# The bucket hash of an attention kernel: one fp32 product on the turned block in place of three split products, and the value product in three parts

## The chip, the cores and the metric

One Trainium2 chip, one core. The time is the device time of one execution in microseconds (us); the kernel before takes 741.85 us, the median of three runs (741.52 to 741.86).

## The reference

Two stages. The first is an attention for 2 batches of 8 heads, 768 positions and 64 columns, in which a query sees only the keys of its own hash bucket:

```python
q_bits = (np.einsum('bhsd,dk->bhsk', q, proj) > 0)          # proj is 64 x 6
k_bits = (np.einsum('bhsd,dk->bhsk', k, proj) > 0)
q_bucket = np.sum(q_bits * 2 ** np.arange(6), axis=-1)       # k_bucket likewise
mask = q_bucket[:, :, :, None] == k_bucket[:, :, None, :]
scores = np.where(mask, q @ k.T / 8, -1e9)
attn = exp(scores - max);  attn = attn / (sum(attn) + 1e-9)
out = attn @ v
```

The second stage takes its output as x (1536 x 512) through 4 experts: `out += p[:, e] * (relu(x @ w1[e]) @ w2[e])`, with w1 512 x 1024 and w2 1024 x 512. Everything is fp32, and the kernel keeps near fp32 by splitting each operand into a high part of reduced precision (fp32r) and the rest, and adding up three products.

## The kernel before, in words

**Order of the work.** Heads are numbered 0 to 15 over both batches. Attention is written as a software pipeline: a step handles 128 queries of one head, so a head has six steps t = 0 to 5, and in step i the stages of several earlier steps are issued in the order of the string `ORDER = "TXSUVMEYNRP"`. The first batch's attention runs alone on the engines (heads 0 to 7, and head 8 with it), then the experts of batch 0 run on TensorE with the attention of batch 1 spread between them, then the experts of batch 1 alone. Each engine executes its own instructions strictly in this written order, and the SP queue issues nearly all transfers in order.

**Stages.** S (`stage_s`): four fp32r matmuls give the scores of 128 queries against 768 keys (`sps`, two banks from the pool `big` with two buffers); VectorE (DVE) takes the row minimum out of them into `p`. E: ScalarE (ACT) takes the exponent. For heads 0 to 8 (`mixed`) T turns `p` with six TensorE transposes into `ptps` (pool `one`, four buffers of one bank), which ACT and DVE copy out; for heads 9 to 15 X and Y turn it by DVE block transposes and a trip through DRAM. V (`stage_v`, L509) multiplies with v: fp32 matmuls, two at a time side by side in the array (`tile_position=(0, g * D)`), into `pv`. U copies `pv` out, M (GpSimd, POOL) applies the denominators. N takes the reciprocal of the denominators `den`, to which E's last step has added 1e-9 on ACT (L410). `LAG_V` says how many steps behind a head's last step V runs: for mixed heads in two parts, at lags 4 and 6 (t = 3 and t = 5 of the next head), for the others in one part at lag 7.

**Preparing a head.** While head x is in work, the generator `prep_head` (from L292) prepares head x+1, one piece per step, at the end of the step (P). It starts from q and k turned so that the 64 columns of q and the 64 of k lie on the 128 partitions. For most heads (`BLOCKS`) DVE does the turning from 32x32 blocks (`turn_blocks`, L288, result `xt`), for heads 0, 1, 9 and 10 TensorE. Then `split_half`: ACT makes the high part `ah` (L230), DVE the rest `al` (L231). POOL copies pieces of these into `q1` and `k2` (L221). TensorE computes the **hash** (L329) as three split products, each in two halves of 384 columns: six matmuls into `hps`, which takes one of the two `big` buffers that the scores use:

```python
for j, (w, a) in enumerate(((phi, ah), (plo, ah), (phi, al))):
    for i, sl in enumerate(halves):
        nc.tensor.matmul(ps[i][:MKE, :NH], w, a[:, sl], start=j == 0, stop=j == 2)
```

ACT takes the sign (L316), POOL makes bit vectors of it (L343) and copies them (L221); they are extra rows of `al` and `k2`, so that the score product itself adds a huge number wherever a bit differs. The first product of head x+1 therefore waits for POOL's last copy. For mixed heads the split is in step t = 0, the hash in t = 2, sign and bits in t = 3.

**Weights.** `load_w` loads expert weights through two buffers on the SP queue, `split_w` splits them (DVE L683, POOL L676), already during the first batch.

Of the kernel before, what the change touches and what calls it, by code (L numbers as in the profile page):

```python
# [18 lines left out]
SGN_SCALE = float(2**20)  # L19
ATT_PACE = 1.0  # L20
LAG_E = 1
LAG_N = 3
LAG_R = ((6, 4), (7, 6))
LAG_T = 3
LAG_X = 2
LAG_Y = 4
LAG_V = ((4, 6), (7,))
LAST_V = (4, 5)
LAG_U = (3, 1)
LAG_M = (10, 10)  # L30
PP_BUFS = 6
TW = 3
QK_AT = 1
BLOCKS = (2, 3, 4, 5, 6, 7, 8, 11, 12, 13, 14, 15)
W_LOAD = 14
W_BUFS = 2
WC = 2
# [12 lines left out]
def tile_lsh_attention__then__domain_moe(  # L50
# [59 lines left out]
    pr = const.tile([P, 2, NB], F32, name="pr")  # L110
    phi_t = const.tile([P, P], F32R, name="phi")
    plo_t = const.tile([P, P], F32R, name="plo")
    phi, plo = phi_t[:, :MKE], plo_t[:, :MKE]
    eps = const.tile([P, 1], F32, name="eps")
# [33 lines left out]

    def setup():
        nc.vector.memset(warm, 0.0)  # L150
        nc.vector.memset(eps, 1e-9)
        nc.scalar.activation(warm[:, 0:1], warm[:, 0:1], ACTF.Exp)
        make_identity(nc, ident)
        keep_warm(N_WARM)
        step_column(qk_scale, ((0, -scale), (D, 1.0)))
        step_column(
            sgn_bias, ((0, -TINY), (MQ + NB, TINY), (MQE, 0.0), (MK, TINY), (MK + NB, -TINY), (MKE, 0.0))
        )
        step_column(bit_mul, ((0, 0.5), (MK, BIG / 2)))
        nc.vector.memset(phi_t.bitcast(F32), 0.0)  # L160
        nc.vector.memset(plo_t.bitcast(F32), 0.0)
        for i, s in ((0, -1.0), (1, 1.0)):
            hi, lo = (
                x[:, MQ:P].rearrange("p (a n) -> p a n", a=2)[:, :, i * NB : (i + 1) * NB] for x in (phi_t, plo_t)
            )
# [21 lines left out]
    def in_blocks(b, h):  # L187
        return b * H + h in BLOCKS
# [100 lines left out]

    def prep_head(b, h):  # L290
        second = (b, h) == (0, 1)
        if not second and not in_blocks(b, h):  # L292
            tqk = loaded.pop((0, b, h))
        q1, al, ah, k2 = stack_tiles(b, h)
        if second:
            for ps, sl in zip(in_psum, halves):
                split_half(ah[:, sl], al[:, sl], ps[:, :NH])
        elif in_blocks(b, h):
            if (b, h) not in xts:
                turn_blocks(b, h)  # L300
                yield 0
            split_half(two(ah), two(al), two(xts.pop((b, h))))
        else:
            ps = big("tps")
            for c in range(NT):
                nc.tensor.transpose(
                    ps[:, c // 3, (c % 3) * P : (c % 3 + 1) * P], tqk[:, c].rearrange("p a d -> p (a d)"), ident
                )
            split_half(two(ah), two(al), ps[:, :, :NH])
        for rows in (slice(0, D), slice(D, P)):  # L310
            copy_pool(q1[rows], ah[0:D].bitcast(F32))
        copy_pool(k2[0:D], ah[D:P].bitcast(F32))
        yield 654

        def sign():
            nc.scalar.activation(  # L316
                two(k2[D:MKE]), hps[D:MKE, :, :NH], ACTF.Sign, bias=sgn_bias[D:MKE], scale=SGN_SCALE
            )

        if mixed(b, h) and (second or in_blocks(b, h)):  # L320
            yield 0
        if second:
            ps = [one("hps1") for _ in range(2)]
        else:
            hps = big("hps")
            ps = [hps[:, i] for i in range(2)]
        for j, (w, a) in enumerate(((phi, ah), (plo, ah), (phi, al))):
            for i, sl in enumerate(halves):
                nc.tensor.matmul(ps[i][:MKE, :NH], w, a[:, sl], start=j == 0, stop=j == 2)  # L329
        copy_pool(ah[0:D], al[D:P].bitcast(F32))  # L330
        if second:
# [4 lines left out]
        if not mixed(b, h):  # L336
            sign()
        yield 978
        if b and h and not in_blocks(b, h):
            yield 0  # L340
        if mixed(b, h) and not second:
            sign()
# [9 lines left out]
        yield 0  # L352

    xhi = {}
    xlo = {}
# [46 lines left out]
    def stage_e(b, h, t):  # L402
        pt, nb = probs_t[b, h, t]
        r, o, n = span_of(b, h, t)
        if o == 0:
            dens[b, h, r] = sm.tile([P, NT], F32, tag="den", name="den")
        nc.scalar.activation(pt, pt, ACTF.Exp, bias=nb, scale=-1.0, accum_out=dens[b, h, r][:, o : o + 1])  # L407
        if o == n - 1:
            den = dens[b, h, r][:, :n]
            nc.scalar.activation(den, den, ACTF.Identity, bias=eps)  # L410

    rdbs = {}
    rows = {}
# [1 line left out]
    def stage_n(b, h, t):  # L415
        r, o, n = span_of(b, h, t)
        if o != n - 1:
            return
        den = dens.pop((b, h, r))
        rd = sm.tile([P, NT], F32, tag="rd", name="rd", bufs=2)  # L420
        nc.vector.reciprocal(out=rd[:, :n], in_=den[:, :n])
        rows[b, h, r] = dr.tile([P, n], F32, tag=f"row{n}", name="row", bufs=6)
        nc.sync.dma_start(out=rows[b, h, r], in_=rd[:, :n])
# [149 lines left out]
    def attention():  # L573
# [3 lines left out]
        def do(op, i):  # L577
# [10 lines left out]
            elif op == "T":  # L588
                j = i - LAG_T
                if 0 <= j < n and heavy(*seq[j]):  # L590
                    stage_t(*seq[j])
                    return 654
            elif op == "X":
                j = i - LAG_X
                if 0 <= j < n and not heavy(*seq[j]):
                    stage_x(*seq[j])
            elif op == "Y":
                j = i - LAG_Y
                if 0 <= j < n and j % G == G - 1 and not heavy(*seq[j]):
                    b, h, t = seq[j]  # L600
                    stage_y(b, h, t // G)
            elif op == "S":
                if i < n:
                    b, h, t = seq[i]
                    if t == 0:
                        x = hseq.index((b, h))
                        prep[0] = prep_head(*hseq[x + 1]) if x + 1 < len(hseq) else iter(())
                    stage_s(b, h, t)
                    return 652 + 4270 // NT
                return DRAIN  # L610
            elif op == "V":
                for bh, lag in ended(i):
                    for part, at in enumerate(v_lags(*bh)):
                        if lag == at:
                            stage_v(*bh, part, len(v_lags(*bh)))
            elif op == "U":
                for bh, lag in ended(i):
                    if lag == u_lag(*bh):
                        stage_u(*bh)
            elif op == "M":  # L620
                for (b, h), lag in ended(i):
                    for g in range(NT // G):
                        if h % 2 and lag == (u_lag(b, h) if (b, h) == (0, H - 1) else LAG_M[b] + g):
# [434 lines left out]
```

## Time and profile before

| | |
|---|---|
| median of three runs | 741.85 us |
| the profiled execution | 741.69 us |
| its span, first to last instruction | 740.0 us |
| TensorE (PE) busy | 720.4 us, 97% of the span |
| DVE, POOL, ACT busy | 474.5, 306.3, 298.9 us |
| mean granted TensorE clock | 0.992 |
| attention of batch 0 and head 8 | to about 152 us |
| experts of batch 0 with attention of batch 1 | 152 to 430 us |
| experts of batch 1 | 430 to 740 us |

A busy share is an average over these three stretches. PE's matmuls are pipelined and their ends are modelled, so durations of PE work are best read from the start of one group to the start of the next. "Idle before" and "waited for" say what an engine stood still for, and what ended it.

### The profile page before, as it was taken

Reading aid. Unit: us, or ns where it says so; the run is one execution under the profiler, and the core shown is the slowest. Engines: PE = TensorE matmul, PEld = TensorE weight load, DVE = VectorE, ACT = ScalarE, POOL = GpSimd, SP = SyncE. Lnnn points to the kernel's source line nnn. Section 1 sums busy time; section 2 is a strip of 40 time slices with the busy share of each in tenths; the row PEclk is TensorE's granted clock in tenths of the full one; section 3 lists DMA queues with packets and bytes.
Section 4 is the critical chain, followed back from the end, with each engine's and each line's share of the span. In section 5 each row is a group of like instructions: output and inputs, shape, how many; then the busy total and the mean of one; then the engine's idle time right before and its main releaser. Section 6 shows DMA issues by size and latency. Waiting matters only on the chain.

```text
span 740.0 us, 10166 instructions
## 1 busy us (share of the span) xinstructions
PE 720.4 (97%) x3826; PEld 618.4 (84%) x3826; DVE 474.5 (64%) x781; ACT 298.9 (40%) x592; POOL 306.3 (41%) x279
## 2 busy tenths in 40 slices
PE   8898889999999999999999999999999999999997
PEld 6666666698897897979779799998989989899896
DVE  6677776545776666667553334798668686676863
ACT  6676767643242241523312010443435334353440
POOL 5338585442335441644132324844234242343420
PEclk9999999999999999999999999999999999999999
DMA  6233324302877797789668211242121221212202
GB/s 143 44 65 66 79 43 101 74 13 69 208 203 177 216 229 189 194 209 280 173 196 231 83 58 57 72 157 85 48 67 58 85 86 34 81 57 78 93 0 86
DMA packets 85504, 83.05 MB, mean 112 GB/s; under 512 B 49872, under 2 KB 52432, under 8 KB 85456
## 3 DMA queue, kind: packets, MB, share of 16 engines
q1 hardware_dynamic: 84432, 82.08, 41.0%
q8 instruction: 30, 0.49, 0.3%
q10 hardware_dynamic: 1024, 0.33, 0.2%
q14 instruction: 18, 0.15, 0.1%
HBM read 62.68 MB, written 19.71 MB: 111 GB/s over the span
## 4 chain that ended last, share of the span: by engine, by line
PE 91%; ACT 4%; DVE 4%; issue 0%; DMA 0%; POOL 0%; DVEq 0%; POOLq 0%
PE mps L715 12%; PE mps L716 12%; PE mps L717 12%; PE pv L509 9%; PE mps L776 6%; PE mps L775 6%; PE mps L777 6%; PE sps L384 3%; PE sps L386 3%; PE ptps L454 3%; PE hps L329 3%; PE mps L930 2%; PE mps L926 2%; PE mps L929 2%; DVE al L231 2%; PE pd L926 2%
## 5 line engine op out<-in xcount | busy, mean ns | idle before, releaser
L715 PE MATMUL mps<-w2hi,hh 128*128 128x512 f32 (+1 forms) x388 | 150.7, 388 | 0.0
L717 PE MATMUL mps<-w2hi,hl 128*128 128x512 f32 (+1 forms) x388 | 150.5, 388 | 0.0
L716 PE MATMUL mps<-w2lo,hh 128*128 128x512 f32 (+1 forms) x388 | 150.4, 388 | 0.0
L391 DVE TENSOR_SCALAR_CACHE_REDUCE p<-sps 128x768 f32<-128x768 f32 x96 | 90.4, 943 | 34.0 <-PE sps L386 32.1
L407 ACT ACTIVATE p<-p,nb 128x768 f32<-128x768 f32 x96 | 89.4, 932 | 37.0 <-DVE p L391 36.5
L709 DVE SCALAR_TENSOR_TENSOR acc<-mps,pe,acc 128x512 f32<-128x512 f32 (+1 forms) x85 | 63.0, 742 | 63.1 <-PE mps L717 62.6
L781 ACT ACTIVATE hh<-mps 128x384 fp32r<-128x384 f32 x64 | 31.4, 490 | 162.3 <-PE mps L777 162.3
L776 PE MATMUL mps<-xs,w1hi 128*128 128x384 f32 x256 | 85.9, 336 | 0.6 <-POOL xs L554 0.6
L775 PE MATMUL mps<-xs,w1hi 128*128 128x384 f32 x256 | 86.4, 337 | 0.0
L777 PE MATMUL mps<-xs,w1lo 128*128 128x384 f32 x256 | 85.9, 336 | 0.0
L717 PEld LDWEIGHTS mps<-w2hi,hl 128*128 128x128 f32 x388 | 72.9, 188 | 15.6
L912 POOL TENSOR_TENSOR w2lo<-ws,w2hi 128x512 fp32r<-128x512 f32 x32 | 40.5, 1286 | 108.4 <-ACT w2hi L911 108.4
L716 PEld LDWEIGHTS mps<-w2lo,hh 128*128 128x128 f32 x388 | 72.9, 188 | 13.8
L715 PEld LDWEIGHTS mps<-w2hi,hh 128*128 128x128 f32 x388 | 72.8, 188 | 13.8
L676 POOL TENSOR_TENSOR w1lo<-ws,w1hi 128x512 fp32r<-128x512 f32 x32 | 42.6, 1332 | 88.3 <-DVE w1hi L683 58.8
L782 DVE SCALAR_TENSOR_TENSOR hl<-mps,hh 128x384 fp32r<-128x384 f32 x64 | 35.4, 555 | 66.6 <-ACT hh L781 66.4
L676 POOL TENSOR_TENSOR w2lo<-ws,w2hi 128x512 fp32r<-128x512 f32 x32 | 41.3, 1289 | 70.5 <-DVE w2hi L683 56.3
L509 PE MATMUL pv<-pt,tv 128*64 128x384 f32 x288 | 67.6, 492 | 0.0
L221 POOL TENSOR_SCALAR q<-ah 64x768 fp32r<-64x768 f32 (+1 forms) x33 | 32.2, 975 | 68.5 <-ACT ah L230 67.2
L384 PE MATMUL sps<-ah,q 128*128 128x384 f32 x192 | 54.6, 365 | 0.3 <-DVE p L391 0.3
L454 PEld LDWEIGHTS ptps<-ident,p 128*128 128x128 f32 x324 | 38.7, 145 | 16.3 <-issue 7.8
L871 POOL TENSOR_TENSOR w1lo<-ws,w1hi 128x512 fp32r<-128x512 f32 x24 | 37.1, 1551 | 36.4 <-ACT w1hi L867 22.7
(135 smaller groups left out, 1430.5 us busy)
## 6 DMA issues: line engine op xcount, KB each, us to landing
ws<-in_moe_w_dram SPq DMA_DIRECT2D x64, 512.0 KB, 4.0
scr<-t SPq DMA_DIRECT2D x14, 1152.0 KB, 8.9
pt<-scr SPq DMA_DIRECT2D x56, 288.0 KB, 6.1
tv<-in_v_dram SPq DMA_DIRECT2D x16, 192.0 KB, 4.3
out_dram<-acc SPq DMA_DIRECT2D x11, 256.0 KB, 2.0
rdb<-row SPq DMA_DIRECT2D x14, 192.0 KB, 5.3
tqk<-in_q_dram SPq DMA_DIRECT2D x26, 96.0 KB, 3.3
tqk<-in_k_dram SPq DMA_DIRECT2D x24, 96.0 KB, 3.4
```

Of the source, the lines that this page charges most:

```text
L384: nc.tensor.matmul(ps[:, i, :NH], q1[:, sl], k1[:, i * NH : (i + 1) * NH], start=True, stop=False)
L391: nc.vector.tensor_scalar(out=two(pt), in0=ps[:, :, :NH], scalar1=MASKED, scalar2=MASKED, op0=ALU.min, op1=ALU.min, accum_out=nb,)
L407: nc.scalar.activation(pt, pt, ACTF.Exp, bias=nb, scale=-1.0, accum_out=dens[b, h, r][:, o : o + 1])
L509: nc.tensor.matmul(dst, vvs[b, h][:, c], pts[b, h, g][c], start=c == 0, stop=c == NT - 1, tile_position=(0, g * D),)
L676: nc.gpsimd.tensor_tensor(out=lo[:, c - 1], in0=st[c - 1], in1=hi[:, c - 1].bitcast(F32), op=ALU.subtract)
L709: nc.vector.scalar_tensor_tensor(out=acc, in0=ps, scalar=pcol, in1=acc, op0=ALU.mult, op1=ALU.add)
L715: nc.tensor.matmul(ps, hh[:, ts], w2hi[:, f, cs], start=n == 0, stop=False)
L716: nc.tensor.matmul(ps, hh[:, ts], w2lo[:, f, cs], start=False, stop=False)
L717: nc.tensor.matmul(ps, hl[:, ts], w2hi[:, f, cs], start=False, stop=n == FC - 1)
L775: nc.tensor.matmul(ps[:, :SB], w1hi[:, kk, fs], xhi[b, kk][:, sl], start=kk == 0, stop=False)
L776: nc.tensor.matmul(ps[:, :SB], w1hi[:, kk, fs], xlo[b, kk][:, sl], start=False, stop=False)
L777: nc.tensor.matmul(ps[:, :SB], w1lo[:, kk, fs], xhi[b, kk][:, sl], start=False, stop=kk == KD - 1)
```

## The change

Five things, all around `prep_head`:

1. The hash of heads 2 to 15 is no longer made of `ah` and `al`, but in fp32 straight from `xt`, with weights `pf` (the projections times their signs and the scale, made once by POOL): two matmuls, one for each half of the columns, side by side in the array and in one bank of the pool `one`. The sign becomes two ACT instructions of 384 columns.
2. The pieces move: for mixed heads `ah` in t = 1, `al` in t = 2, hash, sign and bits in t = 3, the hash directly behind V; for the others `ah` in t = 0, `al`, hash and sign in t = 1, bits in t = 2. The turning on DVE is for all heads in the last step of the head before.
3. Heads 9 and 10 are loaded in blocks and turned by DVE, too.
4. V of mixed heads in three parts at lags 4, 6 and 8, that is in t = 3, 5 and 1; for the others at lag 8, with U at lag 9.
5. 1e-9 is added to the denominators on DVE in N, not on ACT in E.

```diff
+SPLIT_AT = (1, 0)
+HASH_AT = (3, 1)
-LAG_V = ((4, 6), (7,))
+LAG_V = ((4, 6, 8), (8,))
-LAG_U = (3, 1)
+LAG_U = (1, 1)
-BLOCKS = (2, 3, 4, 5, 6, 7, 8, 11, 12, 13, 14, 15)
+BLOCKS = tuple(range(2, 16))
...
+        nc.gpsimd.tensor_copy(sgn_bias[0 : MKE - D], sgn_bias[D:MKE])
+        nc.gpsimd.memset(pf, 0.0)
...
+            nc.gpsimd.tensor_scalar(
+                out=pf.rearrange("p (a n) -> p a n", a=2)[:, :, i * NB : (i + 1) * NB],
+                in0=pr, scalar1=qk_scale, scalar2=s, op0=ALU.mult, op1=ALU.mult,
+            )
...
+            xt = xts.pop((b, h))
+            for _ in range(SPLIT_AT[not mixed(b, h)]):
+                yield 0
+            nc.scalar.activation(two(ah), two(xt), ACTF.Copy, scale=qk_scale)
+            copies()
             yield 0
-        if mixed(b, h) and not second:
-            sign()
+            nc.vector.scalar_tensor_tensor(
+                out=two(al), in0=two(xt), scalar=qk_scale, in1=two(ah).bitcast(F32),
+                op0=ALU.mult, op1=ALU.subtract,
+            )
+            copy_pool(ah[0:D], al[D:P].bitcast(F32))
+            for _ in range(HASH_AT[not mixed(b, h)] - SPLIT_AT[not mixed(b, h)] - 1):
+                yield 0
+            hps = one("hps")
+            for i, sl in enumerate(halves):
+                nc.tensor.matmul(
+                    hps[i * D : i * D + MKE - D, :NH], pf[:, : MKE - D], xt[:, sl],
+                    start=True, stop=True, tile_position=(0, i * D),
+                )
+            for i, sl in enumerate(halves):
+                rows = slice(i * D, i * D + MKE - D)
+                nc.scalar.activation(
+                    k2[D:MKE, sl], hps[rows, :NH], ACTF.Sign, bias=sgn_bias[rows], scale=SGN_SCALE
+                )
...
-        if o == n - 1:
-            den = dens[b, h, r][:, :n]
-            nc.scalar.activation(den, den, ACTF.Identity, bias=eps)
+        nc.vector.tensor_scalar(out=den[:, :n], in0=den[:, :n], scalar1=1e-9, scalar2=None, op0=ALU.add)
         nc.vector.reciprocal(out=rd[:, :n], in_=den[:, :n])
...
-                    if t == NT - 1 and x + 2 < len(hseq) and in_blocks(*hseq[x + 2]) and mixed(*hseq[x + 2]):
+                    if t == NT - 1 and x + 2 < len(hseq) and in_blocks(*hseq[x + 2]):
                         turn_blocks(*hseq[x + 2])
```

The order of TensorE's instructions around a hash of the first batch. Before, in step t = 2 and the next one (`ptps` are the transposes, `sps` the scores, `hps` the hash, `pv` the value product):

```order
L454 MATMUL ptps<-ident,p 128x128 x6
L384 MATMUL sps<-ah,q_372 128x384 x2
L386 MATMUL sps<-k_375,al 128x384 x2
L329 MATMUL hps<-ah,phi 108x384 x2
L329 MATMUL hps<-ah,plo 108x384 x2
L329 MATMUL hps<-al,phi 108x384 x2
L454 MATMUL ptps<-ident,p 128x128 x6
L384 MATMUL sps<-ah,q_372 128x384 x2
L386 MATMUL sps<-k_375,al 128x384 x2
L509 MATMUL pv<-pt,tv 64x384
L509 MATMUL pv<-pth,tv 64x384
```

Of the change, in step t = 3:

```order
L470 MATMUL ptps<-ident,p 128x128 x6
L402 MATMUL sps<-ah,q_374 128x384 x2
L404 MATMUL sps<-k_377,al 128x384 x2
L525 MATMUL pv<-pt,tv 64x384
L525 MATMUL pv<-pth,tv 64x384
L525 MATMUL pv<-pt,tv 64x384
L525 MATMUL pv<-pth,tv 64x384
L346 MATMUL hps<-xt,pf 44x384 x2
L470 MATMUL ptps<-ident,p 128x128 x6
```

Six matmuls that stood alone between two steps are two behind the four of V, and they read `xt` instead of `ah` and `al`.

The same on DVE, from the turning of the next head (`xt`) on. Before:

```order
L288 STREAM_TRANSPOSE xt<-tqk 128x768
L458 COPY pth<-ptps 128x3x128
L391 TENSOR_SCALAR p,nb<-sps 128x768
L231 SCALAR_TENSOR_TENSOR al<-xt,qk_scale,ah 128x768
L683 CAST w1hi<-ws 128x512
L391 TENSOR_SCALAR p,nb<-sps 128x768
L458 COPY pth<-ptps 128x3x128
L391 TENSOR_SCALAR p,nb<-sps 128x768
L536 COPY xf<-pv 64x384
L421 RECIPROCAL rd<-den 128x6
```

Of the change:

```order
L299 STREAM_TRANSPOSE xt<-tqk 128x768
L474 COPY pth<-ptps 128x3x128
L409 TENSOR_SCALAR p,nb<-sps 128x768
L699 CAST w1hi<-ws 128x512
L409 TENSOR_SCALAR p,nb<-sps 128x768
L474 COPY pth<-ptps 128x3x128
L409 TENSOR_SCALAR p,nb<-sps 128x768
L552 COPY xf<-pv 64x384
L436 TENSOR_SCALAR den<-den 128x6
L437 RECIPROCAL rd<-den 128x6
L333 SCALAR_TENSOR_TENSOR al<-xt,qk_scale,ah 128x768
```

`al` moved from behind the scores of t = 0 to behind everything of t = 2, and the small addition to `den` stands ahead of the reciprocal.

POOL's instructions of the change in steps t = 2 to 4 of a head with odd number:

```order
L232 TENSOR_SCALAR ah<-al 64x768
L692 TENSOR_TENSOR w1lo<-ws,w1hi 128x512
L565 TENSOR_TENSOR xf<-xf,rdb 128x384
L567 TENSOR_SCALAR xs_114<-xf 128x384
L570 TENSOR_TENSOR xs_114<-xf,xs_114 128x384
L361 TENSOR_SCALAR al<-k_711,bit_mul 44x768
L232 TENSOR_SCALAR k_711<-al 12x768
```

Their order is the one of before; what moved is the moment from which the first (it needs DVE's `al`) and the sixth (it needs the sign) can run.

## Rows read from the trace of the kernel before

**Rows 1.** Stretches: us, PE, PEld, DVE, ACT, POOL busy (instructions), clock, DMA share, GB/s
```profile
24.82:137.22 112.40, 102.61 (x626) 75.23 (x627) 78.12 (x150) 79.92 (x167) 65.29 (x69) 0.95 0.30 65
...
151.95:430.00 278.05, 278.05 (x1460) 238.94 (x1460) 165.23 (x287) 83.62 (x167) 102.61 (x92) 1.00 0.67 179
430.00:740.00 310.00, 306.19 (x1549) 277.84 (x1547) 205.94 (x290) 109.08 (x205) 117.95 (x81) 1.00 0.21 70
```

**Rows 2.** Waits of PE from 7 to 151 us: total us, times, longest
```profile
PE hps L329 <- DVE p L391: 9.3, 7, 2.1
PE ptps L454 <- ACT pth L460: 1.9, 6, 0.3
PE hps L329 <- DVE al L231: 0.8, 1, 0.8
```

**Rows 3.** The chain that ended last, around one hash: start, us, what
```profile
72.58 1.62 DVE al L231
74.20 0.75 DVE p L391
75.13 1.30 PE hps L329 x6
```

**Rows 4.** The same chain, from two hashes to the next value products
```profile
24.82 2.23 PE hps L329 x6
...
29.01 2.08 PE pv L509 x12
...
41.77 1.31 PE hps L329 x6
...
44.43 2.08 PE pv L509 x12
...
49.38 2.09 PE pv L509 x12
```

**Rows 5.** Stretches behind the same two hashes, columns as in rows 1
```profile
24.82:29.01 4.19, 4.19 (x18) 3.74 (x20) 1.85 (x5) 2.21 (x5) 1.40 (x2) 0.60 0.06 6
41.77:45.96 4.19, 4.19 (x26) 3.05 (x28) 3.92 (x12) 3.31 (x6) 1.50 (x2) 1.00 0.03 5
```

**Rows 6.** Timeline of PE around a value product in the second stretch
```profile
222.72 0.39 PE L716 MATMUL mps<-w2lo,hh 128*128 128x512 f32 x1
222.95 0.39 PE L717 MATMUL mps<-w2hi,hl 128*128 128x512 f32 x1
223.27 4.09 PE L509 MATMUL pv<-pt,tv 128*64 128x384 f32 x24
227.29 0.62 PE L384 MATMUL sps<-ah,q 128*128 128x384 f32 x2
227.74 0.52 PE L386 MATMUL sps<-k,al 76*128 76x384 f32 x2
228.10 0.40 PE L715 MATMUL mps<-w2hi,hh 128*128 128x512 f32 x1
```

**Rows 7.** Timeline of PE: a hash in the second stretch, and what follows it
```profile
163.04 0.50 PE L329 MATMUL hps<-ah,phi 128*108 128x384 f32 x2
...
164.08 0.34 PE L775 MATMUL mps<-xs,w1hi 128*128 128x384 f32 x1
```

**Rows 8.** Timeline of PE: the transposes of head 10, and what follows them
```profile
154.74 0.82 PE L306 MATMUL tps<-ident,tqk 128*128 128x128 f32 x6
155.32 0.42 PE L775 MATMUL mps<-xs,w1hi 128*128 128x384 f32 x1
```

**Rows 9.** Timeline of POOL: first and last of seven instructions without a gap
```profile
59.36 0.83 POOL L221 TENSOR_SCALAR ah<-al 64x768 fp32r<-64x768 f32 x1
...
65.62 0.83 POOL L221 TENSOR_SCALAR k<-al 12x768 fp32r<-12x768 f32 x1
```

**Rows 10.** Waits of the SP queue and of DVE from 150 to 430 us
```profile
SPq L491 <- PE pv L509: 33.5, 6, 7.5
...
DVE w2hi L683 <- DMA ws<-in_moe_w_dram: 7.8, 3, 3.6
```

More of the change, by code (lines that the diff above doesn't have):

```diff
@@ L112, in tile_lsh_attention__then__domain_moe @@
     plo_t = const.tile([P, P], F32R, name="plo")
+    pf = const.tile([P, P - D], F32, name="pf")
     phi, plo = phi_t[:, :MKE], plo_t[:, :MKE]
-    eps = const.tile([P, 1], F32, name="eps")
     warm = const.tile([P, 8], F32, name="warm")
@@ L150, in setup @@
         nc.vector.memset(warm, 0.0)
-        nc.vector.memset(eps, 1e-9)
         nc.scalar.activation(warm[:, 0:1], warm[:, 0:1], ACTF.Exp)
@@ L164, in setup @@
                 x[:, MQ:P].rearrange("p (a n) -> p a n", a=2)[:, :, i * NB : (i + 1) * NB] for x in (phi_t, plo_t)
+            )
+            nc.gpsimd.tensor_scalar(
+                out=pf.rearrange("p (a n) -> p a n", a=2)[:, :, i * NB : (i + 1) * NB],
+                in0=pr,
+                scalar1=qk_scale,
+                scalar2=s,
+                op0=ALU.mult,
+                op1=ALU.mult,
             )
@@ L291, in prep_head, with copies @@
         second = (b, h) == (0, 1)
-        if not second and not in_blocks(b, h):
-            tqk = loaded.pop((0, b, h))
         q1, al, ah, k2 = stack_tiles(b, h)
+        def copies():
+            for rows in (slice(0, D), slice(D, P)):
+                copy_pool(q1[rows], ah[0:D].bitcast(F32))
+            copy_pool(k2[0:D], ah[D:P].bitcast(F32))
         if second:
@@ L297, in prep_head @@
                 split_half(ah[:, sl], al[:, sl], ps[:, :NH])
[L298 to L320, printed above, removed]
+            copies()
+            yield 654
             yield 0
-        if second:
             ps = [one("hps1") for _ in range(2)]
[L324 to L331, printed above, removed]
+            for j, (w, a) in enumerate(((phi, ah), (plo, ah), (phi, al))):
+                for i, sl in enumerate(halves):
+                    nc.tensor.matmul(ps[i][:MKE, :NH], w, a[:, sl], start=j == 0, stop=j == 2)
+            copy_pool(ah[0:D], al[D:P].bitcast(F32))
             for i, sl in enumerate(halves):
@@ L335, in prep_head @@
                 )
-        if not mixed(b, h):
-            sign()
-        yield 978
-        if b and h and not in_blocks(b, h):
-            yield 0
-        if mixed(b, h) and not second:
-            sign()
+            yield 978
+        else:
+            xt = xts.pop((b, h))
+            for _ in range(SPLIT_AT[not mixed(b, h)]):
+                yield 0
+            nc.scalar.activation(two(ah), two(xt), ACTF.Copy, scale=qk_scale)
+            copies()
+            yield 0
+            nc.vector.scalar_tensor_tensor(
+                out=two(al),
+                in0=two(xt),
+                scalar=qk_scale,
+                in1=two(ah).bitcast(F32),
+                op0=ALU.mult,
+                op1=ALU.subtract,
+            )
+            copy_pool(ah[0:D], al[D:P].bitcast(F32))
+            for _ in range(HASH_AT[not mixed(b, h)] - SPLIT_AT[not mixed(b, h)] - 1):
[3 more added lines that the diff above has]
+                nc.tensor.matmul(
+                    hps[i * D : i * D + MKE - D, :NH],
+                    pf[:, : MKE - D],
+                    xt[:, sl],
+                    start=True,
+                    stop=True,
+                    tile_position=(0, i * D),
+                )
+            for i, sl in enumerate(halves):
+                rows = slice(i * D, i * D + MKE - D)
+                nc.scalar.activation(
+                    k2[D:MKE, sl], hps[rows, :NH], ACTF.Sign, bias=sgn_bias[rows], scale=SGN_SCALE
+                )
+            if not mixed(b, h):
+                yield 978
         nc.gpsimd.tensor_scalar(
@@ L351, in prep_head @@
         copy_pool(k2[MQ:MQE], al[MK:MKE].bitcast(F32))
-        yield 0
+        yield 978 if mixed(b, h) and not second else 0
     xhi = {}
```

## The prediction, made before the changed kernel was run

> **What bounds the kernel now.** I cut the span into stretches first [rows 1]. In the second and third, PE is busy nearly all the time (278.05 of 278.05 us, 306.19 of 310.00): there only less PE work counts. In the first, from the hash of head 2 at 24.82 to that of head 9 at 137.22, PE is busy 102.61 of 112.40 us at a clock of 0.95, while ACT (79.92), DVE (78.12) and POOL (65.29) have a third or more to spare. So this stretch is bound by PE plus what PE waits for. The waits come next [rows 2]: the hash L329 stands for 9.3 + 0.8 = 10.1 us of them; nothing else is over 1.9. The chain says why [rows 3]: ACT makes `ah`, DVE then needs 1.62 us for `al`, only behind it takes the minimum of the scores, and that frees one of the two score buffers, for which the hash queues; PE, strictly in order, stands still. Last, the price of what follows [rows 4, 5]: after a wait of about 1 us (hash at 41.77) the six hash matmuls take 1.31 us and the next value product V starts 2.66 us after the hash did, at clock 1.00; after one of about 2 us (24.82) the hash takes 2.23 us and V starts after 4.19 us, at a mean clock of 0.60, so much of that time was at the lower of the two levels, 1.2 instead of 2.4 GHz. Such a dip costs 4.19 - 2.66 = 1.5 us, and there are three (the hashes at 24.82, 58.15 and 107.10).
>
> **The change, part by part.**
>
> *The wait.* The new hash needs `xt`, which DVE made at the end of the head before, and a bank of the pool `one`, not a score buffer. In t = 3 that bank has been free since U's copy in t = 2. So all 10.1 us of [rows 2] can go. I count 9.4: the first of these waits (2.1 us, the longest) ends a piece in which there is no V yet and the other engines set part of the pace. Bounds: 0 if the hash finds another wait, 10.1.
>
> *The hash itself.* Two fp32 matmuls of 384 columns, side by side. The nearest row is V, which has the same shape of moving data and the same placing: 12 such matmuls (24 in the trace, which counts each twice) take 227.29 - 223.27 = 4.02 us [rows 6], 0.67 us a pair. Against 1.31 us [rows 4] that saves 0.64 us at each of the eight hashes in the first stretch (heads 2 to 9): 5.1 us.
>
> *The clock.* With the waits gone there is nothing in front of the three dips: 3 x 1.5 = 4.5 us. Bounds 0 and 4.5; I take 4.5, since the waits of about 1 us at the other hashes were followed by no dip.
>
> *Heads 9 and 10* lose six PE transposes each. In the second stretch they take 155.32 - 154.74 = 0.58 us [rows 8]; 2 x 0.6 = 1.2 us saved. DVE does two more block turnings instead, with 278.05 - 165.23 us to spare [rows 1].
>
> *Hashes in the second stretch.* Six (heads 10 to 15), at 164.08 - 163.04 = 1.04 us now [rows 7]. New: 0.67, plus what it costs to go into and out of the side by side form, as around V [rows 6]: V starts 0.32 us after the matmul before it where 0.23 us is usual (222.95 - 222.72), and the pair behind it takes 0.45 us against 0.36 for the next pair, so 0.09 + 0.09, say 0.19. That is 0.86 and saves 6 x 0.18 = 1.1 us. In the first stretch the hash stands directly behind V and pays no such price.
>
> *V in three parts* does the same multiplications, but enters and leaves that form once more per head: eight heads x 0.19 = 1.5 us lost. Why it could pay: a step is about 1.36 us of PE without V ((4.95 - 2.08 - 0.15) / 2 from 44.43 to 49.38 [rows 4]; 0.15 is my allowance for the way out of V), so V's third part fills t = 1, where ACT now makes `ah`.
>
> *POOL.* The hash moves from t = 2 to t = 3, and `al` from t = 0 to t = 2, but the next head's first product still waits for POOL's last copy. Behind `al`, POOL has seven instructions without a gap in heads 3, 5 and 7, from 59.36 to 66.45: 7.1 us [rows 9], one of them a weight split that is only sometimes there. PE's cover from the start of t = 3 to that product is three steps (4.1), two parts of V (2.8), the hash (0.67) and the transposes ahead of it (about half a step, 0.65): 8.2 us, and `al` ends, as I estimate from its place behind the minimum and the copies of t = 2, about 1 us into t = 3. So 7.1 against 7.2: no slack left. Bounds: 0, or the weight split (about 1.4) and as much again per head. I take 2.2 us lost over the three heads. In the other heads the three multiplications of M are absent and there are some 2 us to spare.
>
> *A wait added on ACT.* Sign now stands in the same step as its hash, so ACT stops until PE is through V and the hash; queued behind it are the copies of the next transposes, which free the banks for PE's transposes after that. PE has waited there up to 0.3 us before [rows 2]. Bounds 0 and 0.3 a head; I take 0.2, over seven heads 1.4 us lost.
>
> *At nothing:* the addition of 1e-9 (14 + 4 small instructions, from ACT to DVE), two Sign instructions for one, the turning one step earlier, POOL's few setup instructions. All lie on engines with a third of the first stretch free and wait for inputs that are there. Heads 9 and 10 get four loads in place of two on the SP queue, issued in the first stretch, where the DMA share is 0.30 [rows 1]. If that cover were gone, it would show as a wait of PE's score product for DVE.
>
> *Sum:* 9.4 + 5.1 + 4.5 + 1.2 + 1.1 - 1.5 - 2.2 - 1.4 = 16.2 us. The profiled execution took 741.69 us, which is 0.2 under the median of the runs; 741.7 - 16.2 = **725.5 us**. With every cost at its low end, the whole first wait, and the 1.9 us of [rows 2] gone too, the gain is 22.4 (719.3); with half of the dips staying and POOL at twice my price or more (5 us), it is 11.2 (730.5).
>
> **The rivals.**
>
> *POOL decides (0.15).* At heads 3, 5 and 7 PE stands about 3 us before the first product, which is long enough for a dip: 3 x (1.6 + 1.5) = 9.3 us instead of 2.2, so 732.6. For it: the train of 7.1 us [rows 9]. Against: only three heads have it, and POOL is free 42% of the stretch [rows 1].
>
> *The two matmuls don't run side by side (0.08).* `pf` has 44 columns, V's weights 64, and if placing depends on that, a hash costs 2 x 0.67 = 1.34 us: 14 x 0.67 = 9.4 us more, 734.9. Against: the place in the array (columns 0 and 64) is given the same way as V's. The Trainium skill has a rule that speaks against the change here: "FP8 and Floating Point Precision", TensorE Precision Notes, counts four passes for a true fp32 product; two such products are eight passes where the six fp32r matmuls of before would be six. V's rows agree as far as that a pair of fp32 matmuls takes about four times the 0.17 us of one fp32r matmul [rows 6, 7], and thus a pair costs what a single one would. By the rule alone, without the pairing, the time would be this rival's.
>
> *Loads queue behind V (0.05), the one on the slower side.* For the light heads V moves from lag 7 to lag 8. In the second stretch the SP queue already stands 33.5 us in six waits for V, because the next `pt` loads need its buffers, and weight loads are queued behind these; DVE has waited up to 3.6 us for weights [rows 10] with PE not losing anything. That stretch holds some 50 steps (seven heads and the drain), so one is about 278 / 50 = 5.5 us. If each of six heads' loads came 5.5 us later and PE's cover were used up, PE would lose 6 x 5.5 = 33 us: 725.5 + 33 = 758. It turns the sign from 16.2 / 6 = 2.7 us a head on. Against: all of `pt`'s loads move with V, so the distance from V to V stays six steps.
>
> *No change (0.04).* The waits come back elsewhere, ACT or DVE setting 16 us a head: with 80 us of work for seven heads they would need 4.6 us of waiting each per head. 740 to 743 us.
>
> **How the numbers follow.** The forecast has 0.68 and its own range, 719 to 731. To reach 8 in 10 the range takes in the POOL rival: 719 to 733, leaving out the unpaired hash, no change and slower, together 0.17. A measurement of this kernel can tell about 0.2%, 1.5 us, from no change: faster 0.91 (forecast, POOL and unpaired), the same 0.04, slower 0.05.
>
> **What would show it.** Right: PE's waits for L329's successor near 0; the new hash about 0.67 us from its start to the next transposes, in the first stretch; the clock at 1.00 from 25 to 137 us; a head in about 14 us instead of 112.4 / 7 = 16.1; the experts' start at about 137 us instead of 152; the third stretch unchanged at 310 us. Wrong in a step: PE waiting for POOL at the first score product of heads 4, 6 and 8; PE's transposes waiting for ACT by more than 0.3 us; a hash of 1.3 us; in the second stretch PE waiting for weights or V for `pt`. The whole is wrong if the first stretch stays over 108 us, or if the second gets longer.

## The result, and the profile after

The changed kernel takes **732.47 us** (median of four runs, 732.15 to 733.85) against 741.68 us of the kernel before on the same chip (738.25 to 741.86): a ratio of 0.989, 95% interval 0.986 to 0.992. It is faster, by 9.2 us where 16.2 were forecast. The kernel before spreads with the granted clock: over the runs beside the experiments it takes 736.5 to 737.4 us at a mean clock of 0.999 and 741.4 to 743.1 us at 0.992 or 0.993; its profiled execution is one of the latter kind. Three stretches and PE's waits tell where the rest went.

Stretches of the changed kernel, columns as in [rows 1]: six heads of the first batch (from the hash of head 2 to that of head 8), the experts of batch 0 (first expert product to the first `pa`, the first product of the experts of batch 1), and the last 310 us:

```profile
25.46:111.95 86.49, 83.09 (x530) 56.35 (x528) 70.72 (x140) 70.18 (x146) 53.08 (x58) 1.00 0.36 74
133.00:479.90 346.90, 339.15 (x1743) 289.06 (x1742) 205.14 (x344) 99.28 (x195) 134.33 (x114) 0.99 0.56 156
422.00:732.00 310.00, 306.53 (x1551) 278.14 (x1549) 205.56 (x290) 108.61 (x204) 118.44 (x81) 1.00 0.22 72
```

The first two of the kernel before, cut at the same points:

```profile
24.82:123.21 98.39, 89.41 (x540) 65.59 (x540) 69.57 (x132) 68.77 (x144) 54.83 (x57) 0.95 0.32 65
148.90:487.60 338.70, 338.10 (x1761) 293.01 (x1760) 200.47 (x335) 100.04 (x197) 136.92 (x114) 1.00 0.59 158
```

Six heads take 86.49 us in place of 98.39, at clock 1.00 in place of 0.95: 14.4 us a head in place of 16.4. ([rows 1] ends at the hash of head 9, which comes a step earlier in its head, so its 112.40 us are somewhat less than seven heads.) The first expert product stands at 133.0 us and not at 148.9: 15.9 us won before it. From the first `pa` to the end of the span both kernels take the same, 252.2 us (479.9 to 732.1) and before 252.4 (487.6 to 740.0). The expert stretch, in which PE has a little less to do, grew from 338.7 to 346.9 us. So 15.9 us came in and 8.2 went out; the profiled executions, 741.69 and 733.85 us, differ by 7.8, somewhat less than the medians.

Waits of PE in the changed kernel from 7 to 430 us (total, times, longest), to be held against [rows 2]:

```profile
PE mps L791 <- DVE hl L798: 5.2, 1, 5.2
PE sps L402 <- DVE p L409: 2.2, 3, 1.2
PE ptps L470 <- DVE pt L474: 1.9, 3, 1.0
PE sps L404 <- POOL k L232: 1.4, 2, 1.3
```

The hash's 10.1 us are gone; no row has the new hash L346 in it. The new first row is one wait of 5.2 us, at 382.27 us, in the expert stretch. Stretches of ten us around it:

```profile
373.00:383.00 10.00, 4.80 (x26) 4.48 (x25) 1.68 (x3) 1.79 (x4) 1.12 (x1) 0.91 0.86 281
383.00:393.00 10.00, 10.00 (x46) 10.00 (x46) 6.09 (x11) 1.48 (x3) 3.99 (x4) 0.75 0.60 125
393.00:403.00 10.00, 10.00 (x46) 8.32 (x45) 3.81 (x7) 0.49 (x1) 2.73 (x3) 1.00 0.57 131
```

In the first of them PE is busy 4.80 of 10 us. In the second it is busy throughout, but at clock 0.75: part of it ran at the lower level, 1.2 GHz. The chain that ended last shows both, and what lies before:

```profile
365.00 3.60 PE pv L525 x22
368.59 0.28 SPq L507
...
370.94 0.53 SPq L496
371.57 9.67 DMA ws<-in_moe_w_dram
381.67 0.56 DVE hl L798
382.27 0.69 PE mps L791
382.96 0.32 PE mps L792
...
387.76 0.31 PE mps L792
388.07 0.18 PE mps L793
```

It reads from the top: V ends; only then can SP issue the four loads of the next turned probabilities (`pt`, L507), whose buffers V was reading; behind them a row and the write of L496; and only then, at 371.57, the weight load `ws`, which lands 9.67 us later. DVE's timeline shows who stood waiting for it:

```profile
381.32 0.43 DVE L699 CAST w2hi<-ws 128x512 fp32r<-128x512 f32 x1 [9.32 <-DMA ws<-in_moe_w_dram]
381.67 0.55 DVE L798 SCALAR_TENSOR_TENSOR hl<-mps,hh 128x384 fp32r<-128x384 f32 x1
```

The cast of the weights waited 9.32 us, and `hl`, which had nothing to do with that load, was queued behind it on DVE. The product at 382.27 waits for `hl`. After the wait the matmuls follow each other at 0.32 us until 388, then at 0.17: (388.07 - 382.27) / 2 = 2.9 us more. So this one event costs 5.2 + 2.9 = 8.1 us. A second one, with the cast at 284.43 (waited 5.62 us), shows as PE's two waits for `p` of 1.8 us together. That makes 9.9 us, against a lengthening of 8.2 us plus the 1.1 us that the stretch should have gained, 9.3. DVE stood 9.3 us and PE 5.2, so about 4.1 us of DVE's wait were covered by work that PE still had (an estimate from these two rows).

Waits of the SP queue and of DVE in the changed kernel from 140 to 430 us, to be held against [rows 10]:

```profile
SPq L507 <- PE pv L525: 43.6, 6, 10.3
...
DVE w2hi L699 <- DMA ws<-in_moe_w_dram: 21.1, 4, 9.3
```

SP waits for V 43.6 us in place of 33.5; DVE waits for weights 21.1 us in place of 7.8.

### The profile page after: what moved, and what is told of

It is laid out like the page before. It is cut to its first block, busy times and chain, and to the rows that moved or that the text cites. A ratio compares the mean times of both kernels' runs of the same rounds, so it can differ in the third digit from the quotient of the medians.

```text
span 732.1 us, 10191 instructions
## 1 busy us (share of the span) xinstructions
PE 713.9 (98%) x3786; PEld 602.3 (82%) x3786; DVE 482.6 (66%) x800; ACT 297.7 (41%) x588; POOL 301.5 (41%) x283
## 4 chain that ended last, share of the span: by engine, by line
PE 89%; DMA 3%; DVE 3%; POOL 2%; issue 1%; ACT 1%; SPq 1%; POOLq 0%; DVEq 0%
PE mps L731 12%; PE mps L732 12%; PE mps L733 12%; PE pv L525 8%; PE mps L791 5%; PE mps L792 5%; PE mps L793 5%; PE ptps L470 4%; PE sps L404 4%; PE sps L402 4%; DMA ws<-in_moe_w_dram 3%; PE mps L946 2%; PE mps L942 2%; PE mps L945 2%; PE pd L942 2%; PE pa L946 2%
## 5 line engine op out<-in xcount | busy, mean ns | idle before, releaser
L791 PE MATMUL mps<-xs,w1hi 128*128 128x384 f32 x256 | 88.1, 344 | 5.3 <-DVE hl L798 5.2
L792 PE MATMUL mps<-xs,w1hi 128*128 128x384 f32 x256 | 87.1, 340 | 0.6 <-POOL xs L570 0.6
L731 PEld LDWEIGHTS mps<-w2hi,hh 128*128 128x128 f32 x388 | 72.8, 188 | 15.1 <-issue 1.2
L928 POOL TENSOR_TENSOR w2lo<-ws,w2hi 128x512 fp32r<-128x512 f32 x32 | 40.5, 1287 | 108.4 <-ACT w2hi L927 108.4
L525 PE MATMUL pv<-pt,tv 128*64 128x384 f32 x288 | 69.1, 494 | 0.0
L791 PEld LDWEIGHTS mps<-xs,w1hi 128*128 128x128 f32 x256 | 48.9, 191 | 9.1 <-DVE hl L798 5.5
L470 PEld LDWEIGHTS ptps<-ident,p 128*128 128x128 f32 x324 | 36.2, 140 | 20.8 <-ACT p L425 9.4
```

The costliest lines, as they stand in the source:

```text
L470: nc.tensor.transpose(ps[:, c * P : (c + 1) * P], pt[:, (a + c) * P : (a + c + 1) * P], ident)
L525: nc.tensor.matmul(dst, vvs[b, h][:, c], pts[b, h, g][c], start=c == 0, stop=c == NT - 1, tile_position=(0, g * D),)
L731: nc.tensor.matmul(ps, hh[:, ts], w2hi[:, f, cs], start=n == 0, stop=False)
L791: nc.tensor.matmul(ps[:, :SB], w1hi[:, kk, fs], xhi[b, kk][:, sl], start=kk == 0, stop=False)
L792: nc.tensor.matmul(ps[:, :SB], w1hi[:, kk, fs], xlo[b, kk][:, sl], start=False, stop=False)
```

## The experiments

Three theories for the 9.3 us. **A**: the light heads' V at lag 8 in place of 7 holds the `pt` loads, and the weight loads behind them on SP come late. **B**: a prepared head now counts fewer units, the planner's total was not changed, and the attention of batch 1 is put denser among the experts. **C**: where the weight loads fall among the others is chance. Diffs are against the changed kernel where nothing else is said.

**One number back: light V at lag 7.**

```
-LAG_V = ((4, 6, 8), (8,))
+LAG_V = ((4, 6, 8), (7,))
```

> One number goes back: the product with V of the light heads (all of batch 1) at lag 7 again, its copies out at 8, as before the change; the rest is the changed kernel. Theory A (the later V holds the loads of the next turned probabilities, and with them the weight loads behind them on SP's queue): the 5.2 us wait at a first-layer matmul at 382 us and the DVE waits for weights (21.1 us in four) shrink to those of the kernel before (longest 7.8 us, PE waits under 1 us), the stretch of experts 0 falls from 346.9 us to 336 to 339, and the whole to 722 to 726 us. Theory B (the attention of batch 1 runs denser among the experts because a prepared head now counts fewer units): lag 7 alone changes nothing, 346 us and 732 us. Theory C (where weight loads fall among the other loads is chance): some other wait of 3 to 6 us appears, 728 to 734 us.

724.87 us, ratio to the kernel before 0.980 (0.976 to 0.984). Its expert stretch, and the waits of SP and DVE:

```profile
132.90:470.50 337.60, 336.99 (x1744) 286.07 (x1741) 203.88 (x344) 99.39 (x195) 133.94 (x114) 1.00 0.59 160
```

```profile
SPq L507 <- PE pv L525: 28.9, 6, 6.6
...
DVE w2hi L699 <- DMA ws<-in_moe_w_dram: 7.1, 4, 3.2
```

```profile
364.61 1.60 SPq L681 DMA_DIRECT2D ws<-in_moe_w_dram  x2
373.78 0.43 DVE L699 CAST w2hi<-ws 128x512 fp32r<-128x512 f32 x1 [3.20 <-DMA ws<-in_moe_w_dram]
```

The last two rows are the same load and the same cast as those at 371.57 and 381.32 above. The load takes about as long here (9.2 us from its issue to its cast, there 9.75), behind the same four `pt` loads and the same write; so the load did not get slower, it was issued 7.0 us later. Of the 4.1 us of cover, 3.2 are in use here, and PE does not wait.

337.6 us: 9.3 under the changed kernel and 1.1 under the kernel before, with PE waiting 0.6 us in all. The first stretch is untouched (first expert product at 132.9). This is A's forecast on each count (its 7.8 us is the total of the waits before, not the longest); B's and C's are not met.

**The planner's total made to agree, V left at lag 8.**

```
-... + H * 1632 + (LAG_M[1] + 2) * DRAIN
+... + H * 978 + (LAG_M[1] + 2) * DRAIN
```

> The planner's total of attention units of batch 1 is made to agree with what a prepared head now yields (978 a head and not 1632), so that the attention of batch 1 is spread wider over the products of the experts; V stays at lag 8. Theory B (denser attention is what delays the weights): the stretch of experts 0 falls from 346.9 us to 336 to 339, the whole to 722 to 726 us. Theory A (the lag of V): the waits of DVE for weights stay at some 20 us and PE's wait of about 5 us stays, 346 us and 731 to 733 us. Theory C: a wait of another size at another place, 728 to 734 us.

735.89 us, 0.994 (0.992 to 0.996). The stretch does not fall, it takes 349.5 us (133.1 to 482.6), and the wait grows:

```profile
PE mps L791 <- DVE hl L798: 7.8, 2, 6.9
```

B falls. A's forecast, 346 us and 731 to 733 in all, is missed on the slower side.

**Both together.**

> Both of these together: V of the light heads at lag 7, and the total of units made to agree. Theories A and B both forecast a stretch of 336 to 339 us and 722 to 726 us in all; if it stays above 342 us, neither is the cause, and the place of the weight loads among the others is (theory C).

725.60 us, 0.982 (0.978 to 0.985), the expert stretch 338.7 us (133.0 to 471.7): close to lag 7 alone, to which the total adds nothing.

**Lag 8 kept, the weight loads issued by ACT.**

```
-        nc.sync.dma_start(out=t, in_=src.rearrange("(k p) f -> p k f", p=P))
+        nc.scalar.dma_start(out=t, in_=src.rearrange("(k p) f -> p k f", p=P))
```

> The changed kernel with the weight loads of the first-batch and second-batch experts issued by ACT and not by SP, so that they no longer stand behind a load that waits. Whether V's lag or the pace made SP's queue late, if SP's order is the channel, the waits of DVE for weights fall from 21.1 us to under 5 us, PE's wait of 5.2 us at 382 us goes, the stretch of experts 0 falls to 336 to 339 us and the whole to 722 to 726 us. If instead the weight buffers come free late (POOL's subtractions), or the transfers themselves share the memory's rate, the waits stay: 730 to 733 us, or more if ACT is held at the issue.

728.92 us, 0.986 (0.982 to 0.991). The expert stretch falls to 336.1 us (134.0 to 470.1) at the later V, and no DVE wait for `ws` is left among the waits that the trace lists. So the queue is the channel: the same late V costs nothing when the weights don't stand behind its followers. The whole was forecast 3 to 7 us lower, and missed: from the first `pa` to the end this kernel takes 255.8 us (470.1 to 725.9) where the one with lag 7 takes 252.2 (470.5 to 722.7). Matmuls show no wait there, but PE's weight loads (PEld) do; at lag 7 they have none in this part:

```profile
PEld mps L731 <- ACT hh L955: 3.2, 7, 0.5
PEld mps L733 <- DVE hl L960: 2.1, 7, 0.3
PEld pd L942 <- ACT mt L981: 1.4, 7, 0.2
```

ACT's timeline shows one of the seven places, first here, then at lag 7 (where the same work stands 0.4 us later):

```profile
485.49 0.37 ACTq L681 DMA_DIRECT2D ws<-in_moe_w_dram  x1
485.91 0.94 ACT L955 ACTIVATE hh<-mt 128x384 fp32r<-128x384 f32 x2 [2.56 <-DVE mt L996]
```

```profile
483.86 0.53 ACT L955 ACTIVATE hh<-mt 128x384 fp32r<-128x384 f32 x1
```

The issue comes right after POOL's subtraction of the weights before (L928), which ends at 485.45; at lag 7 it is SP that waits for this subtraction at the same issue, 124.7 us in 14. The first of the two `hh` now stands behind it, 2.4 us later than at lag 7. So the same thing, work behind a load that waits, has moved from SP to ACT. That the 3.6 us come with the second batch's loads on ACT is shown by a run further down; that they are these waits is read from the trace alone.

**The lag alone, in the kernel before.**

```
-LAG_V = ((4, 6), (7,))
+LAG_V = ((4, 6), (8,))
```

> The kernel before with one number of the change alone: V of the light heads at lag 8 instead of 7 (copies out at 9). If the lag by itself is what costs, the expert stretch (338.7 us before, from the first product of experts 0 to the first `pa`) grows by 5 to 10 us with waits of PE for DVE in it, DVE's waits for weights pass 15 us, and the whole takes 745 to 752 us. If it costs only together with the order that the change gives to the rest of the batch, the stretch stays within 1.5 us and the whole at 740 to 743 us.

746.69 us, 1.0074 (1.0045 to 1.0103): slower, by 5.1 us in the medians and 7.0 in the profiled executions. Its expert stretch is 148.8 to 494.8, 346.0 us in place of 338.7, with these waits:

```profile
PE mps L775 <- DVE hl L782: 3.7, 1, 3.7
...
PE pv L509 <- DVE hl L782: 1.6, 1, 1.6
...
DVE w2hi L683 <- DMA ws<-in_moe_w_dram: 21.5, 6, 8.9
```

The lag does it without anything else of the change.

**One step later still: lag 9.**

```
-LAG_V = ((4, 6, 8), (8,))
+LAG_V = ((4, 6, 8), (9,))
```

> The changed kernel with V of the light heads one step later still, at lag 9. If the lag is the cause by way of SP's queue, a step more (some 5.7 us of the expert stretch) makes it worse: DVE's waits for weights over 30 us, PE's waits in the expert stretch over 15 us, 745 to 765 us. If 8 was a chance collision of one load with another, 9 gives about 725 to 733 us.

763.16 us, 1.029 (1.027 to 1.032). With the run at lag 6 (last experiment) this makes a row of four; all in the expert stretch, us:

| light V at lag | SP waits for V | DVE waits for weights | PE waits for DVE | stretch |
|---|---|---|---|---|
| 6 (V of batch 0 in two parts) | 11.9 | 1.4 | 0 | 340.9 |
| 7 | 28.9 | 7.1 | 0 | 337.6 |
| 8 (the change) | 43.6 | 23.0 | 7.0 | 346.9 |
| 9 | 78.7 | 59.0 | 29.8 | 375.9 |

Over four lags the waits only grow, and lag 8 costs in both kernels: it is no chance collision, and C falls too. (Weights are `w2hi` and `w1hi` together, from the profiled executions; PE waits for DVE only, the 0.6 us for POOL that each of these runs has is left out; at lag 9 PE waits 17.4 + 0.8 us for `hl`, 10.8 for `p`, 0.8 for `xt`.) The price of a step is far from even: from 6 to 7 it gains 3.3 us, from 7 to 8 it costs 9.3, from 8 to 9 29.0.

**The parts that paid.** On top of lag 7, V of the first batch in two parts as before:

```
-LAG_V = ((4, 6, 8), (8,))
-LAG_U = (1, 1)
+LAG_V = ((4, 6), (7,))
+LAG_U = (3, 1)
```

> The light heads' V at lag 7 as in e1, and the product with V of the first batch in two parts as before the change, its copies out at 9: what is left of the change is the hash and its place. The prediction puts 1.5 us of loss on the third part itself (8 heads by 0.19 us) and gives the parts no gain; if that is all, this runs 1.5 us faster than e1, 723 to 724 us, and the expert work starts at 131 to 132 us. If the three parts are what keeps PE from waiting (their gaps stand where the copies of the turned probabilities are awaited), waits come back at the transposes or at the scores, 2 to 8 us, and it takes 727 to 733 us.

**721.85 us**, 0.977 (0.974 to 0.980), the best version measured: the change without its fourth point, the two edits of V. On the same chip the kernel before takes 738.18 us. The first expert product stands at 130.7 us instead of 132.9, the expert stretch is the same 337.6. The third part thus costs 2.2 us where I had 1.5, and it fills no gap that the hash leaves: without it PE's waits are shorter too (transposes for `pt` 1.0 us and not 1.9, scores for POOL 0.7 and not 1.4).

**The two hash products in two banks, not side by side** (lag 7):

```
-            hps = one("hps")
+            hps = big("hps")
...
-                    hps[i * D : i * D + MKE - D, :NH],
+                    hps[: MKE - D, i, :NH],
...
-                    tile_position=(0, i * D),
```

with one Sign over both.

> The kernel e1 (light V at lag 7) with the two hash products of a head in two banks at the same rows, so that they don't stand side by side in one bank. If the pair at 0.65 us runs side by side, each half alone takes 0.65 us and a head 1.31: 14 heads cost 0.65 us each, 9 us in all, 733 to 735 us, some 4 us of it before the first expert product (which then stands at 137 us). If the products followed each other anyway and fp32 costs half of what was taken, nothing changes: 725 us.

730.86 us, 0.989 (0.986 to 0.992): 6.0 above the paired form in the medians, 7.1 in the profiled executions (731.45 and 724.37), and not 9. The chain shows the hash at twice the time, first here, then in the changed kernel:

```profile
25.88 1.28 PE hps L346 x4
```

```profile
25.63 0.65 PE hps L346 x4
```

In the expert stretch six hashes cost 341.4 - 337.6 = 3.8 us, 0.63 each; before it eight cost 136.1 - 132.9 = 3.2 us. (There PE's other waits changed too: those of the transposes fell from 2.6 to 0.7 us, those of the scores for `p` rose from 0.4 to 1.9; what took up the rest of the eight times 0.63 stays open.) The hash stands in a score buffer here and PE still doesn't wait at it, so what took the old wait away is not the bank of the pool `one` that the prediction named beside `xt`; the price of the score buffer may be the 1.5 us more of waits for `p`.

**The six products of before at the new place** (lag 7). The first form changed the computation: the low half's copy into the stack stood ahead of the six products and overwrote the rows of the high half that they read.

> The kernel e1 (light V at lag 7) with the hash in six products of split values as before the change, but at the steps where the change puts it and read by one sign. It separates the shorter hash from its new place. By the prediction's terms the six products take 1.31 us against 0.65, 14 heads by 0.65 us or 9 us, 733 to 736 us, and the waits at the hash stay away because the low halves are ready a step earlier; if it was the fp32 product that took the waits away (it reads only the turned values), the wait at the hash comes back with 0.8 to 2 us a head and the time is 738 us or more.

768.17 us, 1.039 (1.036 to 1.043): PE waited for that copy on POOL at every hash (32.8 us, 14 times), so it says nothing on the question, only what a hash behind POOL would cost. With the copy behind the products, as before the change:

```
-            copy_pool(ah[0:D], al[D:P].bitcast(F32))
...
+            hps = big("hps")
+            for j, (w, a) in enumerate(((phi, ah), (plo, ah), (phi, al))):
+                for i, sl in enumerate(halves):
+                    nc.tensor.matmul(hps[:MKE, i, :NH], w, a[:, sl], start=j == 0, stop=j == 2)
+            copy_pool(ah[0:D], al[D:P].bitcast(F32))
...
```

> The kernel e1 (light V at lag 7) with the hash in six products of split values from a score buffer, as before the change, at the steps where the change puts it; the low half is copied into the stack only after them, again as before. If the place (a step behind the low half) is what took the waits away, the hash has no wait for DVE; it costs 1.31 against 0.65 us, 14 heads, and 730 to 735 us come out. POOL then gets its copy later by about a step, and its train before the next head's first score product can add 1 to 2 us a head: up to 745 us. If it was the fp32 product alone, the waits of about 1 us a head stand at the hash again.

742.84 us, 1.003 (1.001 to 1.006): all of the gain gone. PE's waits:

```profile
PE hps L346 <- DVE al L333: 12.3, 10, 2.3
```

Of the 12.3 us, 9.6 (in five) lie in the expert stretch, where the light heads' hash stands in the step of its `al`; 2.7 are left in the first, where it stands a step behind. So place and kind of product belong together: in the first batch the new place, with the rest of the change as it is, takes most of the wait away (10.1 to 2.7 us), in the second it brings one of 9.6, and of the forms tried only the product that doesn't read `al` has none at either. The first expert product stands at 137.4 us, 4.5 later than with the fp32 pair; the expert stretch takes 353.9 us, with the clock at 0.94 from 220 to 310 us.

**Lag 7 and only the first batch's weights on ACT.**

```
-        nc.sync.dma_start(
+        (nc.scalar if g < NU else nc.sync).dma_start(
...
```

> The kernel e1 (light V at lag 7) with the weight loads of the first batch's experts issued by ACT and those of the second batch by SP. In e1 four casts still wait for weights, 7.1 us on DVE, and none of it reaches PE (no wait for DVE over 0.4 us): so by the reading that only PE's waits count nothing is gained, 724 to 726 us. If those waits still cost PE something that the waits don't name, up to 2 us come off, the stretch of experts 0 going from 337.6 us to 336: 722 to 724 us.

725.57 us, 0.983 (0.979 to 0.986): nothing gained over lag 7, as the waits said. From the first `pa` to the end it takes 251.8 us (471.9 to 723.7), and the changed kernel, with lag 8 and all weights on SP, 252.2; so the 3.6 us lost above came with the second batch's loads on ACT.

**The best version with the light V at lag 6.**

```
-LAG_V = ((4, 6), (7,))
-LAG_U = (3, 1)
+LAG_V = ((4, 6), (6,))
+LAG_U = (3, 2)
```

> The kernel e5 (V of the first batch in two parts, the new hash) with the light heads' V one step earlier still, at lag 6, copies out at 8 as in e5. By the theory that SP waits for V with the weight loads behind it, an earlier V shortens SP's waits (28.9 us in e1) by some 5 us each and DVE's waits for weights (7.9 us in e5) go to about zero; PE has no wait left from these, so the time moves by under 1.5 us, 720 to 723 us. If V at lag 6 comes before its loads have landed, PE waits for DMA in the expert stretch, 2 to 5 us a head over seven heads, 735 to 755 us.

727.74 us, 0.982 (0.979 to 0.985), slower than at lag 7 and between the two forecasts. SP and DVE hardly wait for V and weights any more (table), and PE now waits for the loads themselves:

```profile
PE pv L525 <- DMA pt<-scr: 2.3, 1, 2.3
```

The stretch is 3.3 us longer than at lag 7, 2.3 of it this wait. That is the profiled execution, the fastest of the four (725.27 us, mean clock 1.000); the others take 2.3 to 2.9 us more, at 0.997 or 0.998, and what they spend it on isn't traced. Of the four lags tried 7 is the best: earlier V waits for its own loads, later it holds up those of the weights.

## Why the prediction was right and wrong

**Right: the first stretch as a whole.** The sum without its 1.1 us for the second stretch was 15.1 us, 0.6 of it for the transposes of head 10, which lie behind the first expert product too; 15.9 were measured. The waits at the hash went altogether, and no dip of the clock was left (1.00 over the six heads). That the three dips were worth 4.5 us has no run of its own; the spread of the kernel before with its clock, some 5 us, agrees. Nor has the term of the transposes of heads 9 and 10, 1.2 us. The pair takes 0.65 us where V's rows gave 0.67. A head takes 14.4 us from hash to hash and not about 14, but a head before took 16.4 and not 16.1, so the gain of 2.0 us a head is about the one forecast. POOL's train was dear as forecast in kind, 1.4 us and not 2.2; ACT's wait for Sign cost PE nothing (I had 1.4), but the transposes wait 1.9 us for DVE's copy of `pt`, which I had not named. V's third part was undersized: 2.2 us, not 1.5.

**Right, but hidden: the hashes in the second stretch.** I forecast 1.1 us less; at lag 7 the stretch is 1.1 us shorter than before. But head 10's transposes, 0.58 us [rows 8], have gone out of it as well, so the agreement is in part luck: about 0.5 us are left for the six hashes, and no run sets them apart.

**Wrong: the step on the light heads' lag.** It stood among the rivals at 0.05, and the sum had nothing for it. My reason was that all `pt` loads move with V, so that V to V stays six steps. That is true of `pt` and misses the point, since the weight loads don't move with V. They come when the experts need them, they stand on the same queue, and when SP may go on only a step later, so does whatever is behind: the weight load at 371.57 was issued 7.0 us later than at lag 7. The row to stop at was in [rows 10]: SP already waited up to 7.5 us, and DVE up to 3.6 us for weights. I read the 3.6 us, with PE losing nothing, as slack; it was the sign that the slack, some 4.1 us where it was overrun, was nearly used up. The rival's own price (six heads by 5.5 us) was too high, because only two of the heads held up a weight load by more than its cover: 9.3 us. Priced at two heads by 5.5 us it would have been 736.5 us, still faster than before and not slower. The sign that I had set for the whole to be wrong, a longer second stretch, came: 346.9 us in place of 338.7.

With that step undone the time is 724.87 us, against a forecast of 725.5; the kernel before took 740.74 us beside it, so the gain is 15.9 us of 16.2. In part that is luck: V's third part cost 0.7 us more than the sum had, and the copy of `pt` 1.9 that it hadn't; POOL and ACT together cost 2.2 less.

**The result agrees with a rival that was not at work.** 732.5 is the number of "POOL decides" (732.6). The trace refutes it: PE's score products wait for POOL 1.4 us in all, and the clock shows no dip in the first stretch. Had only the time been looked at, the wrong cause would have seemed proven.

**The unpaired hash** measured 6.0 us (7.1 in the profiled executions) instead of the 9.4 of that rival; the size per hash was right (0.63 in the expert stretch against 0.67), and in the first stretch only 0.4 a hash reached the path.

**"At nothing"** did not quite hold for the addition of 1e-9. On the chain that ended last it stands in the first stretch, ahead of `al`, whose new place this is, and of the copy of `pt` for which the transposes wait longest (1.0 us, until 99.48):

```profile
96.23 0.58 DVE den L436
97.03 1.46 DVE al L333
98.86 0.57 DVE pt L474
```

And it stands there in the backlog behind the late cast at 284 us:

```profile
284.43 0.43 DVE w2hi L699
284.89 0.56 DVE xraw L552
285.48 0.93 DVE den L436
```

0.93 us of DVE time ahead of the `p` for which PE waits (between them the reciprocal and a turning). The cover I had named for it was gone there. What the addition costs by itself was not tried.

## What to carry to other kernels

When a consumer is moved one step later, list every load that stands on a queue behind the loads waiting for its buffers, above all those that do not move with it; a wait of a few us that already shows in an engine off the path may be a margin nearly spent: here 3 to 4 us of some 4. Test each number of a compound change by itself: here one number of the change cost 9.3 us, a second 2.2, and the rest without those two gave what was forecast for the whole (738.18 - 721.85 = 16.3 us). And hold the time that comes out against the waits before believing the theory that predicted it.

## What the runs showed of the hardware that was not expected

A single wait of 5.2 us was followed by 5.8 us of matmuls at about half speed (0.32 us where 0.17 is usual, clock 0.75 over ten us), so that the wait cost more than half its length again.

An addition over 128x6 elements on DVE (L436) is anything but a fixed small price:

```profile
L436 DVE TENSOR_SCALAR den<-den x18: 153/522/1184, 23.6 to 384.0; 128x6 f32<-128x6 f32 x14, 128x3 f32<-128x3 f32 x4
```

Between 0.15 and 1.18 us, median 0.52. In this trace all ten that take over 0.2 us ran beside a POOL instruction; of the other eight, 0.15 to 0.20 us, five ran beside none. That POOL's work lengthens them is thus suggested; no run tests it.

The two late weight loads took 9.67 and 10.79 us until the cast could start (at 371.57 and 273.55), where the median load of weights lands after 3.9 us; the DMA share was 0.86 in the ten us from 373 on. Both stood behind the four `pt` loads and the write that V's end sets off. The first took 9.2 us at lag 7 as well: the burst belongs to both kernels, and the lag decides only when it comes.
